# Two thirds of one chunk's queries transposed by TensorE, and the next chunk's keys by the crossbar in thirds, in a fused attention and MLP kernel

## The chip, the cores and the metric

The kernel runs on one core of a Trainium2 chip. The metric is device time in microseconds (us). TensorE (PE) multiplies matrices, VectorE (DVE) and ScalarE (ACT) work on elements, GpSimd (POOL) and SyncE (SP) mostly issue transfers here. Transfers run on 16 DMA engines. A transfer issued by SP may pass through a crossbar that transposes blocks of 128 x 128.

## The reference

Attention of four batches with eight heads, 768 positions and a head width of 64, followed by a two-layer MLP over all tokens. Three heads are "retrieval" heads with a full causal mask; five are "streaming" heads which keep the first 4 keys and a window of the last 64.

```python
scores = scale * np.matmul(q, k.transpose(0, 1, 3, 2))
mask = np.where(retr, causal, causal & (is_sink | in_window))
a = softmax(np.where(mask, scores, -1e9))
attn = np.matmul(a, v)
x = attn.transpose(0, 2, 1, 3).reshape(B * S, H * D)      # 3072 x 512
h = x @ w_in                                              # 512 -> 2048
out = np.maximum(0.01 * h, h) @ w_out                     # 2048 -> 512
```

## The kernel before, in words

The 3072 tokens are eight chunks of 384, numbered by `ORDER`: a chunk is half of one batch's positions. Chunks 0 to 3 are the first and second halves of batches 0 and 1, interleaved; chunks 4 to 7 those of batches 2 and 3. A chunk is three tiles ("thirds") of 128 positions.

For each chunk GpSimd loads k, q and v by three transfers each, a third at a time, converting from 4-byte to 2-byte numbers (`load_qk`, L119, tiles `kb` and `qb`; `load_v`, L126, tile `va`). `kb` and `qb` have one buffer each, so the load of a chunk's keys waits until the transposes of the chunk before have read the buffer. Scores need q and k with the head width on partitions. From chunk 2 on, `turn_dma` (L242) has SP do this through the crossbar (L248), from `kb` to `kd` and from `qb` to `qd`. Chunks 2 and 3 go in thirds, each one waiting only for its own third's load; from chunk 4 on one transfer takes all three. Chunk 3's last q third is an exception: `turn_third` (L251) has PE transpose it into a PSUM bank, four matmuls with an identity (L254), and ScalarE copies it to `qd` (`move`, L210).

The transposed keys are then "spread" by VectorE (`spreads`, L263): each third is copied twice, the lower and upper 64 partitions to two zero-padded tiles `kt`, one for even and one for odd heads. So there are six copies for each chunk.

`Attention` gives a chunk's work as slots. A slot makes a score block on PE (L355 for retrieval heads, L390 for streaming ones, L335 for the first 4 keys) into a PSUM bank `psS` of which there are two. ScalarE takes the exponential (L360, L395, L338), VectorE masks (L363, L365, L399), and some slots later PE multiplies with v (L324, bank `po`). VectorE divides by the sum (L421, L423, tile `xs`). For chunks up to 2 PE transposes the result (L433) and ScalarE copies it (L435, tile `xt`); from chunk 3 on SP does this through the crossbar (L428).

The MLP's first layer is sixteen steps for each chunk (`in_slots`, L595 on PE, L598 on ScalarE). The second works on pairs of token tiles with seven products in place of eight (`Pair`, units P1 to P7, L765), with sums on VectorE (L748) and additions to partial results (L780); outputs are stored by SP (L777).

All engines run their instructions in the order in which the program writes them[...]. `merge` interleaves MLP steps with attention slots by the steps' costs given in the code. Around the change the order is: `turn_dma(3)`, loads of chunk 4's k, q and v, more MLP steps with the spreads of chunk 2, then chunk 2's attention merged with MLP steps; before its last seven slots comes `turn_third(3, ...)`, after them `spreads(3)`. The loop then starts with n = 2: `turn_dma(4)`, the v shifts of chunk 4 (`v_shift`, L153 and L154), a small load of sink values (L132), loads of chunk 5, and chunk 3's attention merged with chunk 2's first-layer steps; the spreads of chunk 4 stand between its last slots.

Of the kernel before, what the change touches and what calls it, by code (L numbers as in the profile page):

```python
# [12 lines left out]
BF16 = mybir.dt.bfloat16  # L13
# [8 lines left out]
def kernel(  # L22
# [12 lines left out]
    nc = tc.nc  # L35
# [23 lines left out]
    def bank(tag, shape, dtype):  # L59
        return ps.tile(shape, dtype, name=tag, tag=tag, bufs=BANKS[tag])  # L60

    def bf(name, *shape):
        return one.tile([128, *shape], BF16, name=name)
# [5 lines left out]
    ident = bf("ident", 128)  # L69
# [29 lines left out]
    raw = {}  # L99
# [93 lines left out]
    qx = {}  # L193
# [9 lines left out]
    def move(eng, dst, src, hh=None):  # L203

        if eng == "v" and hh is None:
            nc.vector.tensor_copy(dst, src)
        elif eng == "v":
            nc.vector.tensor_scalar_mul(dst, src, half[:, hh : hh + 1])
        elif hh is None:
            nc.scalar.activation(out=dst, in_=src, func=ACTF.Copy)  # L210
        else:
            nc.scalar.activation(out=dst, in_=src, func=ACTF.Copy, scale=half[:, hh : hh + 1])
# [29 lines left out]
    def turn_dma(n):  # L242
        qx[n] = rot.tile([128, 3, 4, 128], BF16, name="qd", tag="qd", bufs=3)
        raw["kx", n] = rot.tile([128, 3, 4, 128], BF16, name="kd", tag="kd", bufs=2)
        for nm, dst in (("k", raw["kx", n]), ("q", qx[n])):
            thirds = [slice(j, j + 1) for j in range(2 if nm == "q" and n == 3 else 3)]
            for g in thirds if n < 4 else [slice(0, 3)]:
                nc.sync.dma_start_transpose(out=dst[:, g].rearrange("p g q t -> p (g q) t"),  # L248
                                            in_=raw[nm, n][:, g].rearrange("p g h d -> p (g h d)"))

    def turn_third(n, tag, eng):  # L251
        pt = bank(tag, [128, 4, 128], BF16)
        for p in range(4):
            nc.tensor.transpose(pt[:, p, :], raw["q", n][:, 2, 2 * p : 2 * p + 2, :], ident[:])  # L254
        move(eng, qx[n][:, 2], pt[:])

    def spreads(n):
        b, c = ORDER[n]
# [14 lines left out]
    def into(slots, extra):  # L273
        r, extra = [], list(extra)
        for j, s in enumerate(slots):
            r.append(s)
            if 5 * j >= 3 * len(slots) and extra:
                r.append(extra.pop(0))
                if len(extra) > len(slots) - j - 2:
                    r.append(extra.pop(0))  # L280
        return r + extra
# [565 lines left out]
    def run(*lists):  # L847
        for l in lists:
            for f in l:
                f()  # L850

    def tail(ms, a):

        n = max(1, (len(ms) - 1) // 3)
        return [a[0], *ms[:n], a[1], *ms[n : 2 * n], a[2], *ms[2 * n :], *a[3:]]

    def merge(ms, as_):

        r, done_, t = [], 0, 0.0
        total = sum(m.us for m in ms)  # L860
        for m in ms:
            t += m.us
            want = round(t / total * len(as_) - 1e-6)
            r += as_[done_:want] + [m]
            done_ = want
        return r + as_[done_:]
# [151 lines left out]
    zero_keys(1, nc.vector, CH, S)  # L1018
    nc.vector.memset(va[2][:, :, :, D], 1.0)
    turn_dma(2)  # L1020
    load_v(2, behind=raw["kx", 2][0:1, 0, 0, 0:1])
    v_shift(2)
# [6 lines left out]
    run(p1[:14], steps(0, ("P1",)), p1[14:])  # L1029
    fourth = weight_sums(1)  # L1030
    turn_dma(3)
    load_qk(4)
    load_v(4)
# [15 lines left out]
    a2, m2, outs = Attention(2, xt_tag="ph").slots([0, (2, 0, 3), 1, (2, 3, 5), 3, 4, 5, 6, 7], lag=3, x=4), m2[:18], m2[18:]  # L1049
    at = last_of(m2, 2.6)  # L1050
    run(merge(m2[:at], a2[:-7]))
    turn_third(3, "psS", "a")
    run(tail(m2[at:], a2[-7:]))
    run(spreads(3))

    for n in range(2, NCH):
        a, extra = [], ()
        if n + 2 < NCH:
            turn_dma(n + 2)
            v_shift(n + 2)  # L1060
            extra = spreads(n + 2)
            if ORDER[n + 2][1] == 0:
                load_sinks(ORDER[n + 2][0])
            if n + 3 < NCH:
                load_qk(n + 3, "k" if n > 2 else "kq")
                if n < 3:
                    load_v(n + 3)
            if ORDER[n + 2][1] == 0:
                sink_values(ORDER[n + 2][0], nc.gpsimd)
        if n + 1 < NCH:  # L1070
            a = Attention(n + 1, cross=True).slots(lag=2 if n > 3 else 3)
            a = into(a, extra) if n > 2 else a
        if n == 4:
            more = [lambda i=i: in_sums(i) for i in range(1, 5)]
            a = [f for j, s in enumerate(a) for f in ([s, more[j // 2 - 1]] if j in (2, 4, 6, 8) else [s])]
# [14 lines left out]
        if n == 2:  # L1090
# [4 lines left out]
            a = a[:-7] + [f for i in range(4) for f in (a[i - 7], *extra[2 * i : 2 * i + 2])]  # L1095
# [49 lines left out]
```

## Time and profile before

| What | Value |
|---|---|
| Median of 3 runs | 225.56 us (224.24 to 225.96) |
| The profiled execution, and its span | 225.19 us, 223.4 us |
| PE, weight loads | 214.9 us (96%), 167.0 us (75%) busy |
| VectorE, ScalarE, GpSimd | 148.4, 135.9, 71.9 us busy |
| Key transposes `kd` by SP | 10, median 7.7 us from issue to landing |
| Query transposes `qd` by SP | 9, median 6.0 us from issue to landing |
| GpSimd idle before loads L119, for `kd` | 31.0 us in 3 waits |
| PE idle before L355, for `qd` | 1.5 us, once |

Times within the profile count from the span's start. An engine's row in a timeline gives start, duration, line, operation, destination and sources, and in brackets the idle time before it with what ended it. The rows of SP and GpSimd's transfers are the time to issue them; the time from issue to landing stands in a separate view. Matmuls overlap in PE's pipeline, so the distance of their starts, and not their durations, says what one costs.

### The profile page before, as it was taken

The numbers are of one execution on the slowest core, as the hardware profiler recorded it, in microseconds if no ns is written. First come the engines' busy times: TensorE is split into PE (matmuls) and PEld (weight loads), VectorE is DVE, ScalarE is ACT, GpSimd is POOL, SyncE is SP. The second block draws the span as 40 slices with busy tenths as digits, with TensorE's granted clock in tenths as the row PEclk, the third lists the DMA queues.
The fourth block names the chain that finished last, engine by engine and source line by source line (L and its number), as shares of the span: only waits on it lengthen the run. The fifth ranks groups of instructions, "written<-read, shape, count | busy, mean of one in ns | idle before, by whom it ended". The sixth has DMA issues, their size and how long they took to land.

```text
span 223.4 us, 5993 instructions
## 1 busy us (share of the span) xinstructions
PE 214.9 (96%) x2404; PEld 167.0 (75%) x2404; DVE 148.4 (66%) x408; ACT 135.9 (61%) x305; POOL 71.9 (32%) x89
## 2 busy tenths in 40 slices
PE   8899999999997999999999999999999999999994
PEld 5578766688885676786687777677787888888893
DVE  6686967849498356972777954355485866847663
ACT  5767947744873997367646553888557785457110
POOL 8997632079206805900619202700000000000000
PEclk9999999999999999999999999999999999999999
DMA  9999999999999999999999993999220041200222
GB/s 129 158 180 169 195 207 179 180 157 156 137 101 217 193 121 189 143 201 123 158 154 156 145 161 121 169 132 157 57 94 4 18 128 22 96 0 3 95 94 94
DMA packets 112683, 29.02 MB, mean 130 GB/s; under 512 B 102672, under 2 KB 109712, under 8 KB 112656
## 3 DMA queue, kind: packets, MB, share of 16 engines
q0 software_dynamic: 77552, 13.37, 85.6%
q1 hardware_dynamic: 34048, 15.01, 38.7%
q8 instruction: 18, 0.29, 0.6%
q10 hardware_dynamic: 1056, 0.26, 0.6%
q14 instruction: 9, 0.07, 0.1%
HBM read 27.30 MB, written 6.29 MB: 150 GB/s over the span
## 4 chain that ended last, share of the span: by engine, by line
PE 68%; DMA 19%; POOL 5%; DVE 4%; issue 1%; SPq 1%; ACT 1%; POOLq 0%; ACTq 0%
PE ph L595 23%; PE py L765 23%; DMA kd<-kb 8%; DMA kb<-in_k_dram 7%; PE po L324 5%; DMA w_in_bf<-in_moe_w_in_dram 4%; PE psS L355 3%; PE po L765 3%; PE psS L595 2%; PE ph L677 2%; POOL kb L119 2%; PE psS L765 2%; POOL va L126 2%; DVE sum L748 1%; PE psS L390 1%; DVE kt L263 1%
## 5 line engine op out<-in xcount | busy, mean ns | idle before, releaser
L595 PE MATMUL ph<-xt,w_in_bf 128*128 128x384 bf16 x384 | 75.4, 326 | 0.1
L598 ACT ACTIVATE g_all<-ph 128x384 bf16<-128x384 f32 x96 | 47.1, 491 | 31.0 <-PE ph L595 29.9
L595 PEld LDWEIGHTS <-w_in_bf 128*128 128x128 bf16 x416 | 37.5, 97 | 18.7 <-issue 0.7
L360 ACT ACTIVATE at<-psS 128x384 bf16<-128x384 f32 x76 | 35.8, 490 | 18.9 <-PE psS L355 17.5
L765 PEld LDWEIGHTS <-sum 128*128 128x128 bf16 x408 | 36.6, 98 | 5.5 <-issue 0.6
L765 PEld LDWEIGHTS <-g_all 128*128 128x128 bf16 x288 | 27.1, 98 | 4.4
L119 POOL DMA_DIRECT2D kb<-in_k_dram x21 | 18.9, 923 | 31.9 <-DMA kd<-kb 31.0
L765 PE MATMUL py<-w_sum,sum 128*128 128x256 bf16 (+1 forms) x184 | 25.6, 270 | 0.2 <-DVE o L780 0.2
L355 PE MATMUL psS<-qd,kt 128*128 128x384 bf16 (+2 forms) x90 | 22.9, 294 | 1.5 <-DMA qd<-qb 1.5
L765 PE MATMUL py<-w_out_bf,sum 128*128 128x256 bf16 (+1 forms) x176 | 24.0, 270 | 0.1
L126 POOL DMA_DIRECT2D va<-in_v_dram x24 | 21.2, 904 | 0.8 <-DMA kb<-in_k_dram 0.4
L119 POOL DMA_DIRECT2D qb<-in_q_dram x21 | 18.9, 915 | 6.1 <-DMA w_in_bf<-in_moe_w_in_dram 2.6
L324 PE MATMUL po<-va,at 128*128 128x65 bf16 x228 | 19.5, 194 | 0.3 <-DVE at L365 0.2
L399 DVE TENSOR_TENSOR ats<-ats,m_win 128x384 bf16<-128x384 bf16 x35 | 12.8, 370 | 9.4 <-ACT ats L395 9.0
L765 PE MATMUL py<-w_out_bf,g_all 128*128 128x256 bf16 x128 | 18.2, 272 | 0.0
L748 DVE TENSOR_TENSOR sum<-g_all 128x1024 bf16<-128x1024 bf16 x25 | 17.1, 683 | 1.7 <-ACT g_all L598 1.6
L324 PEld LDWEIGHTS <-at 128*128 128x128 bf16 x234 | 14.3, 98 | 4.6 <-DVE at L363 0.5
L395 ACT ACTIVATE ats<-psS 128x384 bf16<-128x384 f32 x33 | 15.9, 492 | 2.2 <-PE psS L390 2.0
L263 DVE COPY kt<-kd 64x512 bf16<-64x512 bf16 x36 | 12.1, 337 | 7.5 <-DMA kd<-kb 7.0
L423 DVE TENSOR_TENSOR xs<-po,linv 128x384 bf16<-128x384 f32 x27 | 15.0, 557 | 0.9
L780 DVE TENSOR_TENSOR u<-py,p 128x256 f32<-128x256 f32 x20 | 8.4, 420 | 8.6 <-PE py L765 8.4
L324 PEld LDWEIGHTS <-ats 128*128 128x128 bf16 x210 | 10.1, 98 | 4.0 <-DVE ats L399 1.5
(227 smaller groups left out, 344.2 us busy)
## 6 DMA issues: line engine op xcount, KB each, us to landing
out_dram<-o SPq DMA_DIRECT2D x23, 256.0 KB, 3.4
va<-in_v_dram POOLq DMA_DIRECT2D x24, 128.0 KB, 7.9
kb<-in_k_dram POOLq DMA_DIRECT2D x21, 128.0 KB, 6.2
qb<-in_q_dram POOLq DMA_DIRECT2D x21, 128.0 KB, 7.4
w_out_bf<-in_moe_w_out_dram POOLq DMA_DIRECT2D x4, 512.0 KB, 13.1
w_in_bf<-in_moe_w_in_dram POOLq DMA_DIRECT2D x3, 512.0 KB, 8.7
vb<-va SPq DMA_DIRECT2D x8, 170.6 KB, 5.7
w_in_bf<-in_moe_w_in_dram POOLq DMA_DIRECT2D x2, 256.0 KB, 7.5
```

The costliest lines, as they stand in the source:

```text
L119: nc.gpsimd.dma_start(out=t[:, g], in_=nat[nm][b, c, :, :, g])
L126: nc.gpsimd.dma_start(out=va[b][:, 3 * c + g, :, 0:D], in_=nat["v"][b, c, :, :, g])
L263: nc.vector.tensor_copy(kt[b % 2][hh][r, :, o : o + 128], raw["kx", n][r, g])
L324: nc.tensor.matmul(o, lhsT=lhsT, rhs=rhs, start=first, stop=False, skip_group_check=True)
L355: nc.tensor.matmul(s[:, off : off + w], lhsT=kt[i][hh][:, p, 128 * kj : 128 * kj + 128], rhs=q_of(n, p, lo, CH), start=(j == 0), stop=(j = ...
L360: nc.scalar.activation(out=a[:, 0:off], in_=s[:, 0:off], func=ACTF.Exp, scale=SM)
L395: nc.scalar.activation(out=av_, in_=s[:, 0:CH].rearrange("p (j e f) -> p j e f", j=3, e=2), func=ACTF.Exp, scale=SM)
L423: nc.vector.tensor_tensor(xs[:], po[:, :, :, 0:D], linv.to_broadcast([128, 3, 2, D]), op=ALU.mult)
L595: nc.tensor.matmul(ph[:, 0:CH], lhsT=w_in_bf[:, g, 128 * t : 128 * t + 128], rhs=xts[n][:, g, :] if n else xts[0][:, :, g, :], start=(g == ...
L598: nc.scalar.activation(out=g_all[:, slab(n) : slab(n) + 3, t, :], in_=ph[:, 0:CH].rearrange("p (j t) -> p j t", j=3), func=ACTF.Prelu, alp ...
L748: nc.vector.tensor_tensor(self.s[i], x, y, op=op)
L765: nc.tensor.matmul(s[:, 0 : c1 - c0], lhsT=lhs[:, j, :], rhs=rhs[:, j, c0:c1], start=first and j == 0, stop=(j == NH - 1), skip_group_chec ...
```

## The change

`turn_dma` sends only one third of chunk 3's q through the crossbar instead of two. `turn_thirds` transposes the other two on PE, eight matmuls into one PSUM bank, which ScalarE copies by one instruction. It stands in the same place as `turn_third` did. And chunk 4's keys go through the crossbar by three transfers instead of one, each waiting for its own third's load; chunk 4's q, and all later chunks, stay as they were.

```diff
-            thirds = [slice(j, j + 1) for j in range(2 if nm == "q" and n == 3 else 3)]
-            for g in thirds if n < 4 else [slice(0, 3)]:
+            thirds = [slice(j, j + 1) for j in range(1 if nm == "q" and n == 3 else 3)]
+            for g in thirds if n < 4 or (nm, n) == ("k", 4) else [slice(0, 3)]:
                 nc.sync.dma_start_transpose(out=dst[:, g].rearrange("p g q t -> p (g q) t"),
                                             in_=raw[nm, n][:, g].rearrange("p g h d -> p (g h d)"))

-    def turn_third(n, tag, eng):
-        pt = bank(tag, [128, 4, 128], BF16)
-        for p in range(4):
-            nc.tensor.transpose(pt[:, p, :], raw["q", n][:, 2, 2 * p : 2 * p + 2, :], ident[:])
-        move(eng, qx[n][:, 2], pt[:])
+    def turn_thirds(n, gs, tag, eng):
+        pt = bank(tag, [128, 2, 4, 128], BF16)
+        for j, g in enumerate(gs):
+            for p in range(4):
+                nc.tensor.transpose(pt[:, j, p, :], raw["q", n][:, g, 2 * p : 2 * p + 2, :], ident[:])
+        move(eng, qx[n][:, gs[0] : gs[0] + len(gs)], pt[:, 0 : len(gs)])
...
-    turn_third(3, "psS", "a")
+    turn_thirds(3, (1, 2), "psS", "a")
```

## The prediction

> **What bounds the kernel now.** I read the page's busy times first, then the table of stretches of 4 us, and only then the timelines of single engines around the stretches in which TensorE (PE) is not full. The share of busy time names the bound:
>
> ```profile
> PE 214.9 (96%) x2404; PEld 167.0 (75%) x2404; DVE 148.4 (66%) x408; ACT 135.9 (61%) x305; POOL 71.9 (32%) x89
> ```
>
> PE is full, so only its holes can be won back. The stretches say where they are (columns: busy us and count of PE, weight loads, VectorE, ScalarE, GpSimd):
>
> ```profile
> core 0: us, PE busy (x) PEld busy (x) DVE busy (x) ACT busy (x) POOL busy (x), PEclk, DMA share, GB/s
> 68.00:72.00 4.00, 2.50 (x23) 1.79 (x21) 3.02 (x8) 1.37 (x3) 2.85 (x4) 1.00 1.15 240
> ...
> 88.00:92.00 4.00, 3.60 (x37) 2.77 (x36) 3.72 (x12) 0.71 (x2) 3.56 (x5) 1.00 1.93 150
> 92.00:96.00 4.00, 3.82 (x45) 2.95 (x43) 3.55 (x7) 2.43 (x6) 3.46 (x4) 1.00 2.29 131
> ```
>
> From 56 us on PE misses 1.50 us in the first row, 0.40 and 0.18 in the last two, 0.15 at 56 to 60 and 0.08 at 144 to 152: 2.3 us is all that these edits could ever win there. PE's timeline says what it waited for (the bracket is idle time and releaser):
>
> ```profile
> 71.03 0.34 PE L355 MATMUL psS<-qd,kt 128*128 128x384 bf16 x1 [1.50 <-DMA qd<-qb]
> ...
> 88.76 0.20 PE L324 MATMUL po<-vb,ats 128*128 128x65 bf16 x1 [0.33 <-DVE ats L399]
> ```
>
> The first is the first score of chunk 3, waiting for its q; PE had been ready at 71.03 - 1.50 = 69.53. The second waits for a mask on VectorE. Who made these late stands in SyncE's (SP's) issues and in the chain of waits, where "DMA" is the time from issue to landing:
>
> ```profile
> 53.84 5.41 SPq L248 DMA_TRANSPOSE kd<-kb  x3
> 59.35 4.13 SPq L248 DMA_TRANSPOSE qd<-qb  x2
> ...
> 78.88 1.56 SPq L248 DMA_TRANSPOSE kd<-kb  x1
> 81.49 3.38 SPq L248 DMA_TRANSPOSE qd<-qb  x1
> ...
> 87.71 5.16 SPq L428 DMA_TRANSPOSE xt<-xs  x4
> ```
>
> ```profile
> 57.56 10.66 DMA kd<-kb
> ...
> 70.66 8.07 DMA kb<-in_k_dram
> 78.88 6.59 DMA kd<-kb
> ```
>
> Chunk 3's two crossbar q thirds are issued at 59.35 and 61.99 and land 9.7 and 9.0 us later by the landing view: 69.05 and 70.99. The second is the wait. For chunk 4, the last key load lands at 70.66 + 8.07 = 78.73; only then the one transpose of all keys starts, and it lands at 78.88 + 6.59 = 85.47. VectorE stands for it, with a mask queued behind it:
>
> ```profile
> 69.91 2.39 DVE L263 COPY kt<-kd 64x512 bf16<-64x512 bf16 x6
> ...
> 85.49 0.59 DVE L263 COPY kt<-kd 64x512 bf16<-64x512 bf16 x2 [2.40 <-DMA kd<-kb]
> ...
> 88.34 0.36 DVE L399 TENSOR_TENSOR ats<-ats,m_win 128x384 bf16<-128x384 bf16 x1
> ```
>
> **What the Trainium skill says.** "DMA: Bandwidth & Descriptors", section "Issuing engines are not separate DMA queues": transfers from SP and GpSimd share the same engines and interleave. The trace agrees: a third issued at 59.35 takes 9.7 us beside the loads, and the same third at 42.7, with less around it, 3.8. Same page, "Queues, rings and completion order": one queue's descriptors are consumed in ring order on each engine. That fits landings in issue order (68.22, 69.05, 70.99), and I rest on it below: removing the last one does not pull in those ahead. "PSUM — Partial Sum Buffer", "Specifications (TRN2)": a bank holds 2 KiB per partition. Two thirds are 2 x 4 x 128 elements of 2 bytes, exactly one bank, so no further bank is taken.
>
> **Part 1: one more third of chunk 3's q through PE.** Removed: the SP issue at 61.99, and with it the landing at 70.99. The remaining third lands at 69.05. PE's added work is four transposes with their weight loads. The present four start at 65.30 and the next matmul at 65.52: 0.22 us, so +0.22 (upper end, if weight loads set the pace: 4 x 98 ns = 0.39; lower end 0). Their operand, the third load of q's middle third, landed near 61, over 4 us ahead. ScalarE's copy grows from 512 to 1024 columns: 384 columns take 0.48 and 512 take 0.60, so 128 cost 0.12 and the copy costs about 1.08, +0.46. Queued behind it is one L435 copy (66.22 to 66.70), after which ScalarE idles 1.39 until 68.09. That hides it; without this cover, PE's L433 at 68.77, which reuses the bank, would be 0.46 late. PE comes to the first score at 69.53 + 0.22 = 69.75, later than 69.05: the whole 1.50 goes, net +1.28.
>
> What is late next: chunk 3's key spreads. VectorE's six copies start at 69.91 behind an addition that waits for PE, so they move to 70.13, 0.4 us each. The group of keys 4 and 5 (at 73.01, 1.98 after the first score) needs the fifth copy, done at about 70.13 + 5 x 0.40 = 72.13; PE would come at 69.75 + 1.98 = 71.73. I take a stall of 0.4 (from 0, if copies are as short as the 0.29 of the lone ones, to 0.6). Part 1 leaves 1.28 - 0.40 = 0.88.
>
> SP is free 2 us sooner at 61.5, so two stores of 256 KB start sooner; they stay behind the keys in the ring. GpSimd's loads of chunk 4's q (71.88) wait no more for the q third that landed at 70.99, and come 0.3 sooner; its k loads still wait for keys landing at 68.22. Neither VectorE nor GpSimd gets another instruction.
>
> **Part 2: chunk 4's keys in thirds.** SP issues three transposes where it issued one, each behind its own load. By issue times and the landing view the loads land at 73.7, 78.0 and 78.7. The first third goes out at about 73.9; SP is idle then, its stores being issued by 70.8. The other two go from 78.0, each 1.3 to 1.8 to issue (chunk 3's three took 5.41). Whole, the work took 6.59 from issue to landing, 2.2 a third; with one third already out, the last lands at about 78.0 + 1.5 + 2 x 2.0 = 83.5 instead of 85.47 (from 82.5 to 86.0, a loss of 0.5, if three issues back up the queue). VectorE's wait is per third now, so the first two copies need not wait at all. In PE's new time it reaches them at 83.1 - 0.9 = 82.2. Waiting for the last pair until 83.5, it ends the copies near 84.5, where the mask at 88.34 - 0.9 = 87.4 is no longer behind them. The hole of 0.33 closes, and of the 0.18 at 93.26, VectorE's backlog from these copies, I take all: +0.51. At worst nothing.
>
> Also freed: chunk 5's k loads (at 86.02 on GpSimd, waiting for 85.47) start 2 us sooner. PE has no hole for them to fill until 144.
>
> Behind SP's extra issues (2 x 1.5 = 3 us more) stand chunk 4's q, two v shifts, the sinks and chunk 3's four output transposes (xt, 87.71). The 1.56 at 78.88 becomes two issues from 78.0 to about 81; the q issue waited for its own load until 81.49 anyway. So I book zero. The cover is thin: the last xt is issued at 91.62 and lands 6.7 later at 98.3, PE needs it at 98.90 now and at 97.5 after a gain of 1.4. The queue must be 0.8 us sooner there; with the keys landed, q's 3.38 of issue should shrink by about 1.
>
> **The sum.** +1.50 - 0.22 - 0.40 + 0.33 + 0.18 = 1.39, say 1.4 us. The profiled execution took 225.19 (span 223.4), so it becomes 223.8. The median of the runs shown is 225.56, 0.37 above it, so I forecast 224.2.
>
> **Rivals.**
> - *The next wait takes most of it.* Key spreads stall 0.6, or SP's xt lands where it did and PE waits for it: 98.3 against 97.5 costs 0.8. For: xt's issues come back to back behind a q issue of 3.38. Against: q's load sets that issue's start. Gain 0.4 to 0.8: 225.0.
> - *All holes close.* Spreads at 0.29 each stall nothing, the hole of 0.08 goes too: 1.9 us, 223.7. For: the keys 2 us sooner. Against: VectorE is 3.02 of 4 busy just there.
> - *Slower: SP's queue slips.* Should the key thirds take 2.5 us each to issue (q issues took 2.53 at 61.99, 3.38 at 81.49), the last ends at 83.0, q at 86.4 and the last xt is issued at 93.2, landing at 99.9. It decides from 0.6 us of slip on. PE, due at 97.5, waits 2.4: 1.0 slower, 226.5. Against: the crossbar is emptier at 74 to 78 than in those cases.
> - *The change doesn't do what it says.* Out: the changed kernel's instruction lists show four more transposes on PE, one q issue fewer and two key issues more on SP, the first score waiting for one q transfer, and each pair of key copies for its own third.
>
> **How the numbers follow.** Forecast 0.55, next wait 0.25, all holes 0.10, slower 0.10. The runs shown spread over 224.24 to 225.96, and about 1% (2.26 us) is what a measurement here can tell from no change. No case reaches that by itself, the holes hold 2.3; faster by over 1% (below 223.3) needs the better cases and a low draw, 0.14. Slower by over 1% (above 227.8) needs the slipped queue and more, 0.04; within 1%, 0.82. The range 222.8 to 226.0 holds the first three cases with the scatter of the runs; the likeliest one's own is 223.2 to 225.2.
>
> **What would show it.** PE's row at 68 to 72 near 3.6 instead of 2.5, with no wait for q; a short wait for a key copy near 72; the L210 copy at about 1.05; key thirds issued at 74 and 78 to 81; VectorE's wait for keys about 1 us or less, ended by 84; no wait for ats at 87. Wrong: PE waiting for xt near 98, or chunk 3's keys landing later than 68.2.

## The result, and the profile after

| | Before | Changed |
|---|---|---|
| Median, 20 runs each | 225.91 us (224.24 to 226.88) | 225.81 us (224.44 to 229.32) |
| The profiled execution, its span | 225.19, 223.4 us | 224.96, 223.2 us |

The ratio of the times is 1.0001 (0.9977 to 1.0025): no difference. The forecast of 1.4 us in 225.6 is a ratio of 0.9938, which lies outside the interval. The median does lie within the stated range of 222.8 to 226.0, but only because that range also held the scatter of the runs. The ratios here and below leave out runs more than about 1.5% above the fastest of their kernel, so they can differ from the quotient of the medians.

The busy times of the changed kernel (line numbers are one higher from L256 on):

```profile
PE 214.8 (96%) x2408; PEld 167.1 (75%) x2408; DVE 148.8 (67%) x408; ACT 136.5 (61%) x305; POOL 71.6 (32%) x89
```

Four matmuls more, and otherwise the same work. The stretches (busy us and count by engine) show that the holes moved:

```profile
core 0: us, PE busy (x) PEld busy (x) DVE busy (x) ACT busy (x) POOL busy (x), PEclk, DMA share, GB/s
56.00:60.00 4.00, 3.37 (x48) 2.57 (x47) 1.54 (x6) 2.75 (x7) 1.39 (x2) 1.00 2.09 146
...
68.00:72.00 4.00, 4.00 (x42) 3.19 (x39) 3.00 (x8) 2.10 (x6) 3.14 (x4) 1.00 1.01 276
72.00:76.00 4.00, 3.38 (x40) 2.15 (x39) 2.76 (x8) 3.10 (x8) 4.00 (x6) 1.00 1.74 168
...
88.00:92.00 4.00, 3.93 (x44) 3.16 (x41) 2.89 (x7) 0.98 (x2) 4.00 (x6) 1.00 1.51 124
92.00:96.00 4.00, 3.96 (x50) 3.13 (x48) 3.54 (x8) 2.70 (x7) 3.34 (x4) 1.00 2.38 145
```

The 1.50 at 68 to 72 is gone, and of the 0.40 and 0.18 at 88 to 96 there is 0.11 left. There is 0.62 at 72 to 76, where PE was full, and 0.63 at 56 to 60, ahead of everything that the change touches. PE's timeline names both:

```profile
56.99 0.27 PE L325 MATMUL po<-va,at 128*128 128x65 bf16 x3 [0.63 <-DVE at L366]
...
70.43 0.33 PE L356 MATMUL psS<-qd,kt 128*128 128x384 bf16 x1
...
73.44 0.23 PE L356 MATMUL psS<-qd,kt 128*128 128x128 bf16 x1 [0.62 <-DVE kt L264]
```

The wait for q is gone at the first score of chunk 3, and a wait for its key spreads stands 3 us later.

The chain that ended last no longer runs through chunk 3's and 4's transposes and loads. The page's summary of it:

```profile
PE 82%; DMA 7%; POOL 4%; DVE 4%; issue 1%; ACT 0%; POOLq 0%
```

After 50 us it has no transfer at all; before, the three of 57.56, 70.66 and 78.88 took 25.32 us of it. A chain can lose a ninth of the span in this way and end 0.2 us sooner, since PE is busy beside it.

I matched the same PE instructions of the two traces one to one and took the start after minus the start before. It is +0.84 at 56, +1.06 at 65.5 (behind the added transposes), -0.60 at the first score, +0.33 at 73.3, -0.18 at 88.8, -0.31 at 93, and -0.18 at the end. Between these two executions, what the change touches won 1.02 us: +0.22, -1.66 at q, +0.93 at the spreads, -0.51 at the mask. And 0.84 was lost up to 56, ahead of everything that the change touches, which is nearly as much. One pair of traces can't say which of these figures belong to the kernels and which to one execution. That is what the experiments ask first.

### The profile page after: what moved, and what is told of

The parts are those of the page before. It is cut to its first block, busy times and chain, and to the rows that moved or that the text cites. A ratio compares the mean times of both kernels' runs of the same rounds, so it can differ in the third digit from the quotient of the medians.

```text
span 223.2 us, 6005 instructions
## 1 busy us (share of the span) xinstructions
PE 214.8 (96%) x2408; PEld 167.1 (75%) x2408; DVE 148.8 (67%) x408; ACT 136.5 (61%) x305; POOL 71.6 (32%) x89
## 4 chain that ended last, share of the span: by engine, by line
PE 82%; DMA 7%; POOL 4%; DVE 4%; issue 1%; ACT 0%; POOLq 0%
PE ph L596 28%; PE py L766 26%; PE po L325 7%; PE psS L356 5%; DMA w_in_bf<-in_moe_w_in_dram 4%; DMA kb<-in_k_dram 3%; PE po L766 3%; PE psS L596 2%; PE psS L391 2%; PE ph L678 2%; POOL va L126 2%; PE psS L766 2%; DVE kt L264 1%; DVE sum L749 1%; PE po L678 1%; PE psS L678 1%
```

## The experiments

Ratios are to the kernel before on the same chip, with a 95% interval. All lines keep the numbering of the kernel that they come from.

**The two kernels once more.** The first run is the kernel before, with no edit.

> The kernel before, unchanged, for a second execution's trace. Theory A (the wait for q was long in the one execution shown, and is shorter as a rule): PE's wait for q before the first score of chunk 3 is at most 1.0 us here, not 1.50, because PE comes there later while the transfers do not. Theory B (the holes are as they were seen, and what they give is taken back at the crossbar transposes of chunk 3's output): the wait is again 1.3 to 1.7 us, and PE reaches chunk 3's first layer 0.3 to 0.9 us after the last output transpose has landed.

It took 226.66 us (span 224.9). Its PE timeline:

```profile
71.82 0.60 PE L765 MATMUL py<-w_sum,sum 128*128 128x256 bf16 x4
72.53 0.34 PE L355 MATMUL psS<-qd,kt 128*128 128x384 bf16 x1
```

The bracket with 1.50 is missing: PE idled for 0.12 us, and by the distance of the starts (0.71, where 0.44 is the distance without a wait) it lost 0.27. So A is right: the wait isn't a property of the kernel. PE arrived at the first score at 72.4 here, and at 69.5 in the first trace, while q landed at 72.48 instead of 70.99. From 50 us on the whole trace runs 1.5 us later, and q with it. PE lost the rest ahead of the score, 0.62 at 58.15 and, in this trace alone,

```profile
62.79 0.19 PE L324 MATMUL po<-vb,ats 128*128 128x65 bf16 x1 [0.99 <-DVE ats L399]
```

The profile names a mask. In the first trace the same product ran 0.7 us ahead of that mask, so the shifted v (`vb`) that it also reads, the last part of which arrived at 62.66, is likelier. The time that PE lost there it did not have to wait for q. The changed kernel, run once more at the end together with the runs on `kb`:

> The changed kernel unchanged, for a second trace. By the present theory: no wait for q, a stall of 0.4 to 1.0 us for the key spreads near 73 us, no hole near 88 us, the last key third of chunk 4 landing at 84.5 us or later, and VectorE waiting 4 us or more for chunk 5's keys near 105 us, with or without a hole of up to 0.6 us on PE.

```profile
74.65 0.23 PE L356 MATMUL psS<-qd,kt 128*128 128x128 bf16 x1 [0.62 <-DVE kt L264]
```

226.18 us (span 224.4). The stall on the spreads came again to the hundredth, and keys in thirds landed at 87.3. What the change costs recurs in the second trace of its kernel; what it was to remove did not recur in the second trace of before.

**Each part alone.** Part 1 is the diff shown above with `if n < 4` left as it was. Part 2 is only

```diff
-            for g in thirds if n < 4 else [slice(0, 3)]:
+            for g in thirds if n < 4 or (nm, n) == ("k", 4) else [slice(0, 3)]:
```

> The first part of the change alone: two thirds of chunk 3's q through PE, chunk 4's keys in one transfer as before. Theory A: no wait for q, +0.22 us of transposes, a stall of 0.6 to 1.0 us for the key spreads near 73 us; over the runs a ratio of 0.998 to 1.002. Theory B: the same up to 73 us, 0.3 to 0.9 us ahead of before at 80 us, the hole of about 0.3 us for the mask near 88 us stays or grows, and near 98 us PE waits for the output transposes for the rest; ratio 0.997 to 1.000.

> The second part alone: chunk 4's keys in thirds, q as before. Both theories: nothing changes up to 84 us, the wait for q stays; the first key third is spread before the others have landed, the last lands no sooner than 85.5 us, and the hole near 88 us closes. Theory A: 0.3 to 0.6 us shorter, ratio 0.997 to 0.999. Theory B: the gain is lost again near 98 us, where PE waits for the output transposes; ratio 0.999 to 1.002.

Part 1 took 225.88 against 225.81, ratio 1.0013 (0.999 to 1.0036), with a stall of 0.49 on the spreads at 74.81. Part 2 took 226.70, ratio 1.0013 (0.9985 to 1.0042). Neither shows a gain: the intervals leave room for 0.2 and 0.3 us at most, so no large gain of one is there for the other to eat. Part 1 came out as theory A said, with a stall a little shorter. Part 2 missed A's ratio, and the wait for q, which both theories expected to stay, didn't. Theory B's wait near 98 us came in neither. Part 2's trace, with q as before, has these lines of PE:

```profile
70.36 0.33 PE L355 MATMUL psS<-qd,kt 128*128 128x384 bf16 x1
...
73.02 0.23 PE L355 MATMUL psS<-qd,kt 128*128 128x128 bf16 x1 [0.42 <-DVE kt L263]
...
106.88 0.27 PE L324 MATMUL po<-va,at 128*128 128x65 bf16 x3 [0.57 <-DVE at L363]
```

There is no wait for q though two thirds still go through the crossbar, and here the spreads stall PE without part 1. The two waits lie on the same stretch, and a long first one hides the second. A new one stands at 106.88, behind chunk 5's key copies (VectorE):

```profile
105.91 0.59 DVE L263 COPY kt<-kd 64x512 bf16<-64x512 bf16 x2 [5.08 <-DMA kd<-kb]
...
106.53 0.29 DVE L363 TENSOR_TENSOR at<-at,m_caus 128x256 bf16<-128x256 bf16 x1
```

**Chunk 3's spreads earlier.** The six copies go ahead of the last half of P7, first in the changed kernel, then in the kernel before:

```diff
-    run(tail(m2[at:], a2[-7:]))
-    run(spreads(3))
+    ends = tail(m2[at:], a2[-7:])
+    run(ends[:-5], spreads(3), ends[-5:])
```

> The changed kernel with chunk 3's six key spreads moved on VectorE ahead of the addition and sum of the last P7 step, so that they start when the keys land (about 68.3 us). Both theories: the stall of 0.9 us near 73 us goes. Theory A: 0.7 to 0.9 us shorter than the changed kernel, ratio to the kernel before 0.995 to 0.998. Theory B: PE then waits 0.5 to 0.9 us near 98 us for the output transposes of chunk 3, and the ratio stays at 0.999 to 1.001.

> The kernel before with only chunk 3's key spreads moved ahead of the last P7 step's addition and sum; neither part of the change. Theory C (the standing wait is the one for the key spreads; the wait for q of the execution first shown is no rule, PE comes to the first score about when q lands): the stall near 73 us goes, the wait for q is at most 0.4 us, and the ratio is 0.996 to 0.999, as with the change. Rival D (early spreads pay only because the change has moved q's landing out of the way): PE now waits 0.5 us or more for q before the first score, and the ratio is 0.999 or above.

VectorE in the first of the two, and PE in the second:

```profile
69.09 2.39 DVE L264 COPY kt<-kd 64x512 bf16<-64x512 bf16 x6
71.51 0.42 DVE L781 TENSOR_TENSOR u<-py,p 128x256 f32<-128x256 f32 x1
```

```profile
69.65 0.60 PE L765 MATMUL py<-w_sum,sum 128*128 128x256 bf16 x4
70.09 0.33 PE L355 MATMUL psS<-qd,kt 128*128 128x384 bf16 x1
```

The copies start at 69.09 instead of 70.97, and the stall is gone. The ratios are 0.9975 (0.9949 to 1.0001) with the change, in theory A's range, and 1.0007 (0.9972 to 1.0043) without it, on 14 runs, which misses theory C's. The intervals overlap, so what the early copies are worth stays inconclusive; both traces are of the shortest execution of their kernel, and don't settle it. In the kernel before PE has neither wait: it goes from P7 to the first score in 0.44. So the trace is as theory C said, and rival D's wait for q isn't there.

**A fixed piece of work as a yardstick.** In the loop's first turn `outs` has six steps. Its first two stand in `lead`, and `outs[-6:]` takes them again, so P5's two halves are computed twice: eight matmuls of 0.109 us, with a sum and an addition on VectorE. The repeat is taken out of the kernel before, then of the changed kernel with early spreads, then of the kernel before with early spreads:

```diff
-            ms = lead + merge(ins[2:], outs[2:-6]) + outs[-6:]
+            ms = lead + merge(ins[2:], outs[2:-6]) + (outs[2:] if n == 2 else outs[-6:])
```

> The kernel before without the second run of pair 2's P5, which its order repeats near 89 us: the same output, 8 matmuls of 0.109 us, one addition and one sum less. Both theories: 0.87 us less on PE. Theory C: all of it is kept, 0.6 to 1.1 us shorter, ratio 0.995 to 0.998, and the trace again shows no wait for q above 0.4 us. Rival D: PE waits again near 71 us for 1.0 to 1.6 us for q; the ratio is as under C, since this work lies after the wait.

> The changed kernel with early key spreads and without the repeated P5. Theory C: the two gains add, 1.3 to 1.7 us shorter than before, ratio 0.992 to 0.995. Rival E (PE meets the next transfer, chunk 3's output transposes near 98 us): PE waits there for 0.5 us or more and the ratio is 0.995 to 0.998.

> The kernel before with early key spreads and without the repeated P5; neither part of the change. Theory C: the change is worth nothing here either, ratio within 0.002 of that of the changed kernel with both edits. Rival D: q and the keys are needed earlier here and the change is worth 0.5 us or more, ratio at least 0.002 higher, with waits for q near 71 us.

| Kernel | Median, us | Ratio |
|---|---|---|
| Before, once | 224.44 | 0.9962 (0.994 to 0.9984) |
| Changed, early spreads, once | 225.15 | 0.9965 (0.9942 to 0.9989) |
| Before, early spreads, once | 224.15 | 0.9945 (0.9917 to 0.9973) |

Eight matmuls are 0.87 us, or 0.39%. In the kernel before 0.38% came (0.16 to 0.60), so the runs can tell a change of this size. With early spreads the difference of the ratios is 0.62% in the kernel before and 0.10% in the changed one, each uncertain by some 0.4%; that such work is always kept whole isn't shown. The edit isn't only eight matmuls less, either: `merge` places attention slots by their share of the steps' cost, so in all four traces without the repeat (the fourth is below, with two buffers) chunk 3's fourth score follows the third at once, where four first-layer matmuls (L595) stood between them, and PE waits 0.34 there. The second kernel missed theory C's range of 0.992 to 0.995. It lost 0.63 at 105.95, behind a mask, as part 2 alone did; rival E's wait for xt isn't in its trace. The third kernel has nothing of the change and the lowest ratio of all; it is 0.0020 below the second, the edge of what theory C allowed, and rival D's gain isn't there (the intervals overlap, so no more is said). Its first score, PE's timeline:

```profile
70.71 0.60 PE L765 MATMUL py<-w_sum,sum 128*128 128x256 bf16 x4
71.15 0.33 PE L355 MATMUL psS<-qd,kt 128*128 128x384 bf16 x1
...
72.71 0.32 PE L355 MATMUL psS<-qd,kt 128*128 128x384 bf16 x1 [0.34 <-DVE kt L263]
```

No wait for q here either. The 0.34 is the wait of the new order: here the profile puts it down to a key copy, in two of the other three traces to ScalarE, which empties the score banks.

**A second buffer for the raw keys.** If the key thirds' gain is lost because chunk 5's k loads still wait for the last third to free `kb`, a second buffer should free them:

```diff
-            t = rot.tile([128, 3, H, D], BF16, name=f"{nm}b", tag=f"{nm}b", bufs=1)
+            t = rot.tile([128, 3, H, D], BF16, name=f"{nm}b", tag=f"{nm}b", bufs=2 if nm == "k" else 1)
...
-                    (("p1s", "kd", 2), ("us", "kd", 2), ("u3s", "kb", 1))]
+                    (("p1s", "kd", 2), ("us", "kd", 2), ("u3s", "kb", 2))]
```

The tiles `blank` and `diff` move into the buffers of the sums to make room; that move was not run on its own. The edit is put into the changed kernel, the kernel before, and the best version.

> The changed kernel with two buffers for the loaded keys, so that a chunk's k loads no longer wait for the transposes of the chunk before (two small constants move to a shared buffer to make room). Theory F (what the key thirds give near 88 us is taken back near 106 us, because the last third lands later and chunk 5's k loads wait for it): chunk 5's k loads are issued by 80 us instead of 86.5, VectorE's wait for chunk 5's keys near 105 us shrinks by 2 us or more, no hole on PE near 106 us, ratio 0.996 to 0.999. Rival G (the buffer was what kept loads out of the way): chunk 4's k loads, now issued near 57 us, crowd chunk 3's transposes, its keys land later than 69 us, PE waits 0.5 us or more near 71 to 74 us; ratio 1.000 or above.

> The kernel before with the same two key buffers. Theory F: little to win, as chunk 5's keys have made no hole near 106 us in the executions of kernels with whole key transposes; ratio 0.998 to 1.001. Rival G: q lands later than 71 us and PE waits for it by 0.5 us or more; ratio 1.001 or above.

> The kernel before with early key spreads, without the repeated P5, and with two key buffers. Theory F: 0.2 to 0.6 us better than without the second buffer, ratio 0.991 to 0.994, since the holes near 88 us (0.5 us in that kernel's trace) close with earlier keys. Rival G: chunk 3's keys land later than 69 us, the spreads are late again and PE waits near 72 us; ratio 0.996 or above.

The ratios are 1.0059 (1.0032 to 1.0085), 1.0051 (1.002 to 1.0082) and 1.0057 (1.0025 to 1.009): each 1.2 to 1.3 us slower than the kernel before, the last one 2.5 us slower than without the buffer by the difference of its ratios, 0.0112. Theory G's ratios came in all three, theory F's in none. G's place came in the kernel before; the trace of the changed kernel (229.56 us) isn't used here. In the kernel before with two buffers, GpSimd issues chunk 4's k loads at once, beside chunk 3's transposes, and PE waits for q (GpSimd, then PE):

```profile
57.43 1.78 POOL L119 DMA_DIRECT2D kb<-in_k_dram  x2
59.92 0.88 POOL L119 DMA_DIRECT2D kb<-in_k_dram  x1 [0.72 <-DMA qb<-in_q_dram]
```

```profile
71.66 0.34 PE L355 MATMUL psS<-qd,kt 128*128 128x384 bf16 x1 [1.23 <-DMA qd<-qb]
```

In the best version with two buffers, chunk 3's key copies start at 69.63, no later than without the second buffer, and the waits come at chunk 4, for q and for the v of the sink positions (`vs`, which GpSimd makes):

```profile
92.31 0.32 PE L355 MATMUL psS<-qd,kt 128*128 128x384 bf16 x1 [0.63 <-DMA qd<-qb]
...
99.39 0.22 PE L324 MATMUL po<-vs,at_sink 128*128 128x65 bf16 x2 [1.73 <-POOL vs L136]
```

The times say that the single buffer, which holds loads back, is worth more here than it costs. That it does so by keeping loads away from the transposes is read from these traces only; the 1.23, taken alone, is no larger than the 1.50 of before's first trace.

## Why the prediction was wrong, step by step

**The step that failed** is the first term of the sum, "the whole 1.50 goes, net +1.28". The mechanism was right, q's third did leave the path, but the size came from one execution. Of six traces with two crossbar thirds and one `kb` buffer, PE's idle time before the first score is 1.50 in the first, 0.12 in the second one of the same kernel, and 0 in the other four: part 2 alone, early spreads, no repeat, and both of these. The mean is 0.27, and the 0.22 of the transposes with the longer stall on the spreads uses that up. Part 2 alone and the kernel without the repeat run the same instructions as the kernel before up to that score, so four executions of the same stretch gave 1.50, 0.12, 0 and 0. Two things met in the first trace. PE came early, since its hole at 56 was 0.16 where every other trace has 0.6 to 0.8. And q landed late: at 70.99, against 68.16 with early spreads and 68.68 without the repeat, where PE came only 0.7 and 0.8 us later. In both traces of before q's second third landed about 2 us behind the third ahead of it, in the traces with early spreads, without the repeat, and with both 0.4 to 0.6. PE's 0.22 for the transposes, by contrast, is paid in every execution.

Two readings of the prediction were off beside it, without weight in the sum. The issue of 2.53 us is that at 59.35, the one at 61.97 took 1.51. And 3.8 us is the median of chunk 2's three q thirds from 42.7 to 46.3; the one at 42.7 took 5.1.

**Key spreads, "a stall of 0.4".** Right in place, too small in size: 0.62 by the bracket, 0.93 by the starts. The copies were taken at 0.40 each; they took 2.74 for six, which is 0.46. Five are as long as in the first trace, the first took 0.62 instead of 0.28. That GpSimd's issues stretch them is likely, not shown (VectorE of the changed kernel, then of the kernel before with two `kb`, in which GpSimd issues nothing from 61 to 72.17):

```profile
70.97 2.74 DVE L264 COPY kt<-kd 64x512 bf16<-64x512 bf16 x6
```

```profile
70.81 1.88 DVE L263 COPY kt<-kd 64x512 bf16<-64x512 bf16 x6
```

And it isn't caused by part 1 alone: it is what shows once q isn't late. By the starts the late spreads cost nothing in the first trace of before, 0.2 in the second, and 0.6 with part 2 alone; with PE's second third they cost 0.9, 0.7 and 1.1.

**The mask's hole, +0.33 and +0.18.** The first closed, by another way than the sum said. "The last lands at about 83.5" failed: it landed at 85.9, later than the whole transfer's 85.47, though its load had landed at 76.85 and not at 78.73. SyncE's issues, and the view of landings by tile (the line with x3 gives the issue times in ns, the next one the landing times):

```profile
75.06 3.99 SPq L248 DMA_TRANSPOSE kd<-kb  x3
79.89 5.11 SPq L248 DMA_TRANSPOSE qd<-qb  x1
```

```profile
L248 SPq DMA_TRANSPOSE kd<-kb x3: 1225/1261/1320, 75.1 to 77.7; - x3
...
DMA to landing us min/median/max: 8.2/8.6/8.9
```

The issue times were as predicted or better, 1.3 a third. The landings weren't: 8.9 us for the first third and 8.2 for the last (the trace doesn't tell the middle one's), where 2 us a third behind the first were booked. What did help is that VectorE finishes the first two pairs before the last lands:

```profile
84.03 0.59 DVE L264 COPY kt<-kd 64x512 bf16<-64x512 bf16 x2 [0.60 <-DMA kd<-kb]
85.43 0.59 DVE L264 COPY kt<-kd 64x512 bf16<-64x512 bf16 x2 [0.56 <-DMA kd<-kb]
86.26 0.58 DVE L264 COPY kt<-kd 64x512 bf16<-64x512 bf16 x2
86.88 0.36 DVE L400 TENSOR_TENSOR ats<-ats,m_win 128x384 bf16<-128x384 bf16 x1
```

The mask runs at 86.88 instead of 88.34. Over all traces with one `kb`, the last key third lands at 84.5 to 87.3 (mean of five 86.0), the whole transfer at 82.9 to 86.1 (mean of six 85.1): the end of the transfer isn't earlier. Counted from the landing of the last load, it is 7.7 to 10.5 us for thirds and 6.7 to 8.4 for the whole. Holes between 87 and 94 come to 0.22 to 0.57 in the six traces with the whole transfer, and to no bracket in the five with thirds.

**"PE has no hole to fill until 144"** failed, and its sign with it. Chunk 5's k loads wait for the last landing, so they start at 86.50 (GpSimd), not 2 us sooner than 86.02:

```profile
86.50 2.63 POOL L119 DMA_DIRECT2D kb<-in_k_dram  x3 [9.68 <-DMA kd<-kb]
```

Two of five traces with thirds have a hole near 106, 0.57 and 0.63, behind chunk 5's key copies or the mask after them; none of six with the whole transfer has. That the later loads cause it is only argued. The second buffer takes their wait away, but changes so much else that it doesn't test this.

**What held.** The transposes cost 0.22, to the hundredth. ScalarE's larger copy took 1.02 (predicted 1.08), and ScalarE had 0.97 idle after it:

```profile
66.78 1.02 ACT L210 ACTIVATE qd<-psS 128x1024 bf16<-128x1024 bf16 x1 [0.15 <-PE psS L255]
67.70 0.48 ACT L436 ACTIVATE xt<-ph 128x384 bf16<-128x384 bf16 x1
69.15 0.38 ACT L790 ACTIVATE o<-ph 128x256 f32<-128x256 f32 x1 [0.97 <-PE ph L766]
```

SyncE's queue didn't slip into PE's way, though q's issue took 5.11 where I expected it to shrink from 3.38. The cover at xt is as thin as I wrote: without the repeat, where PE is earlier, PE waited 0.30 for xt at 98.19. The rival that the next wait takes most of it named the right place and 0.6 us; it too started from 1.28 that aren't there as a rule.

**The account by the starts.** Brackets leave out waits below 0.15 us, so I also take the distance between the starts of matmuls that all these kernels have. They start at 65.19 (the last one ahead of the transposes of chunk 3's q), 73.27, 85.06, 98.90 and 110.07 in the first trace. From 73 to 85 all eight traces take 11.8 us.

| Trace | 65 to 73 | 85 to 99 | 99 to 110 | 65 to 110 |
|---|---|---|---|---|
| Before | 8.08 | 13.84 | 11.17 | 44.88 |
| Before again | 6.90 | 13.54 | 11.17 | 43.40 |
| Part 1 alone | 7.29 | 13.26 | 11.17 | 43.51 |
| Part 2 alone | 7.01 | 13.07 | 12.05 | 43.91 |
| Changed | 7.58 | 13.20 | 11.30 | 43.86 |
| Changed again | 7.69 | 13.19 | 11.30 | 43.96 |
| Before, early spreads | 6.41 | 13.50 | 11.17 | 42.87 |
| Changed, early spreads | 6.63 | 13.20 | 11.17 | 42.78 |

The forecast was 43.5 for the last column. The second trace of before has 43.40 with no change at all. From 65 to 73, where part 1 works, the three traces with late spreads and without it have 7.33 on the mean, the three with it 7.52: nothing gained. With early spreads, where PE waits neither for q nor for keys, part 1 costs 0.22, its transposes. From 85 to 99 part 2 does gain, 0.4 on the mean of four traces each, but from 99 to 110 it loses 0.3; together 24.6 with the thirds against 24.7 with the whole transfer. These are few traces, and the runs decide: their interval allows a gain of 0.5 and a loss of 0.6 us, and excludes 1.4. Ahead of 50 us the eight traces already differ by up to 2.0 us, behind 110 by 0.05.

**What stays open.** Why q landed about 2 us behind the third ahead of it in both traces of before, and 0.4 to 0.6 in three others. Whether early spreads alone gain. What makes the hole near 106. How much of the second buffer's loss is the moved tiles'.

## What to carry to other kernels

A wait read in one profiled execution is one draw: when it depends on how two streams of transfers fell, take the same kernel's trace two or three times before pricing an edit by it, while work added to the full engine is paid in every one of them. Waits on the same stretch didn't add up here; ask what the consumer would have waited for next, and price the removal by the difference only. Cutting the key transfer in pieces moved its first landing forward (80.8 to 84.0 instead of 82.9 to 86.1), not its last one, so it helps a consumer that can start with a piece, and not a buffer that comes free with the last.

## What the hardware showed

- Chunk 3's key copies of 64x512 on VectorE take 0.28 to 0.29 us with GpSimd quiet, and up to 0.62 in the changed kernel and 0.73 in its second trace while GpSimd issues loads. Not every issue stretches one: in the kernel before with two `kb` the last two copies, beside the q loads issued from 72.17 on, stayed at 0.28 and 0.29. The Trainium skill, "SBUF — State Buffer", section "Who interferes with whom", says that VectorE in some modes and GpSimd share a pair of ports and that the one that comes second is blocked until the first is done. The traces fit in that VectorE's copies stretch, here by up to 0.45; that it is this lock was not tested.
- The first and the last third (128x512 each) of chunk 4's keys through the crossbar took 7.6 and 10.2 us to land in the changed kernel's second trace, the whole of three 6.6 in the kernel before. Less data didn't land sooner.
- A second buffer for the keys, which lets loads start sooner, left three kernels 0.5 to 0.6% slower than the kernel before.
